# Attention decode block: other loads for W_o's last head, V, W_gate and x, and group ends placed one step later

## Chip, cores and metric

The kernel runs on one core of one Trainium2 chip. The metric is the device time of one execution in microseconds (us). Three runs gave 660.15, 661.10 and 661.72 us, so the median is 661.1 us.

## What is computed

One decode step (one token) of a pre-norm block for a batch of two: attention over a cache, then a gated MLP.

```python
h  = x + attention(layernorm(x))           # x: [2, 1, 512]
#   q = x @ wq: 32 heads of 128;  k_cache, v_cache: [2, 32, 8192, 128], bf16
#   p = softmax(q k^T * 128**-0.5);  o = p v;  attention = o @ wo     (wo: [4096, 512])
h2 = h + (relu(n @ W_gate) * (n @ W_up)) @ W_down      # n = layernorm(h), F = 1376
```

The two caches hold 268 MB and every byte is used once. With the weights, 281 MB are read.

## The kernel before, in words

**Tiling.** K and V are read in tiles of four heads of one batch element ("quads"): 128 partitions x 64 KB, 8.4 MB each. There are 16 such groups. Steps 0 to 14 take one quad each (Q is step 14, `LASTQ`); the last group is cut into two pairs of heads, p0 and p1, whose tiles have 4.2 MB.

**Buffers.** Three buffers of 64 KB a partition (`bufs`) serve all tiles in rotation. V of step i+1 goes where K of step i was, and is issued by SyncE (SP) after `scores(i)` on VectorE (DVE). K of step i+2 goes where V of step i was, and is issued after `values(i)` on TensorE (PE). At the end the same buffers take W_o, W_gate, W_up and W_down.

**A step.** `scores_pe` does the last 24 to 32 of the step's 256 blocks of keys with PE and ScalarE (ACT). `products` (L378, DVE) multiplies the other blocks with q in place, and `scores` (L396, L398, DVE) sums them by halving. `largest_of_own` and ACT (L418) make the exponentials, and `place_own` (L423, DVE) lays them out in `pgq`. `values` (L449) is 64 matmuls with V.

**Groups of heads.** After steps 3, 7, 11 and 14 (`groups`), `diagonals` collects up to 16 heads' outputs in `o_ps`. `close(i)` ends a group one step later. It multiplies the sums out (`own_sums`, L299, DVE), adds them over partitions (`sums`, L308, PE), takes the reciprocal (`shares`, L312, DVE) and scales (`normalise`, L316, DVE). In step i+1 it stands behind `place_own` and the first eight matmuls of `values`. For group 11, in step 12, `spread` (L484, DVE) and `lay_rows` (L495, L497) follow. They turn heads 0 to 15 into the rows that W_o's set 0 needs.

**The order on each engine** is the order of the code (`tc.manual_schedule()`). So a DVE instruction that waits for PE holds all DVE work behind it.

**Loads.** All loads but x are issued by SP. Each load takes the next of eight completion semaphores, and its issue waits until the load eight places before it has landed. At the end SP issues in this order: V of p0, W_o set 0, V of p1 in four pieces (L588), W_o sets 1 to 3, W_o's heads 30 and 31 in one load (L591), W_gate in two, W_up in two, W_down in seven (L619). The lines that the change replaces there:

```python
load_tile(A_v_cache, p1, p1.vt, pieces=4)
...
nc.sync.dma_start(
    out=wo[:, HM * D:Hq * D].rearrange("p (h n) -> p h n", n=D),
    in_=_dram(A_wo, HM * Dh * D, [[D, P], [Dh * D, Hq - HM], [1, D]]),
)
```

**After the last step** come the pairs: `values_cols(p1)` (L472), `attend_set` (L505) and `attend` for heads 30 and 31 (L512). Then come the second layernorm, W_gate and W_up (L673), the residual (L701), W_down (L712), `y` (L717), a transpose and the store (L723).

Of the kernel before, what the change touches and what calls it, by code (L numbers as in the profile page):

```python
# [18 lines left out]
def _dram(t, offset, dims):  # L19
    return bass.AP(tensor=t.tensor, offset=t.offset + offset, ap=[list(d) for d in dims])  # L20
# [3 lines left out]
def kernel(  # L24
# [13 lines left out]
    nc = tc.nc  # L38
    P = nc.NUM_PARTITIONS
    B, Sq, D = A_x.shape  # L40
    _, Hkv, Sk, Dh = A_k_cache.shape
    Hq = A_wq.shape[1] // Dh
# [26 lines left out]
    HM = 30  # L69
# [53 lines left out]
    xr = bufs[2][0:B, HALF + Hq * Dh:HALF + Hq * Dh + D]  # L123

    wo = bufs[0][:, HALF:TILE]
# [32 lines left out]
    Q = LASTQ  # L158

    def load_tile(cache, s, dst, pieces=1):  # L160
        h = NH * s.g + (0 if s.quad else 2 * s.k)
        n = s.nt * Dh
        w = n // pieces
        for k in range(pieces):
            nc.sync.dma_start(
                out=dst[:, k * w:(k + 1) * w], in_=_dram(cache, (s.b * Hkv + h) * Sk * Dh + k * w, [[n, P], [1, w]]),
            )
# [18 lines left out]

    with tc.manual_schedule():

        nc.scalar.dma_start(out=xr, in_=_dram(A_x, 0, [[D, B], [1, D]]))
        nc.sync.dma_start(out=bufs[2][:, 0:HALF], in_=_dram(A_wq, 0, [[KC * Hq * Dh, P], [1, KC * Hq * Dh]]))  # L190
        load_tile(A_k_cache, steps[0], steps[0].kt)
        load_tile(A_v_cache, steps[0], steps[0].vt)
# [6 lines left out]
            out=nscale, in_=nscale, compare_op=ALU.not_equal, fill=-SCALE,  # L199
# [5 lines left out]
            out=ident_f, in_=ident_f, compare_op=ALU.not_equal, fill=1.0,  # L205
# [4 lines left out]
            out=sel, in_=sel, compare_op=ALU.not_equal, fill=1.0,  # L210
# [9 lines left out]
            out=pick, in_=pick, compare_op=ALU.not_equal, fill=1.0,  # L220
# [24 lines left out]
        for g0 in range(0, NQ, 4):  # L245
            for n0 in range(NH * g0 * Dh, NH * (g0 + 4) * Dh, 4 * Dh):
                q_ps = ps2.tile([B, 4 * Dh], f32, tag="o")
                for c in range(KC):
                    nc.tensor.matmul(  # L249
                        out=q_ps, lhsT=xn[:, c, :], rhs=wq_sb[:, c, n0:n0 + 4 * Dh], start=(c == 0), stop=(c == KC - 1),  # L250
# [46 lines left out]
        def own_sums(i):  # L297
            b, g0, n = groups[i]
            nc.vector.tensor_tensor(  # L299
                out=zc[:, b, g0:g0 + n, :], in0=_free(zs, b * NQ + g0, [[1, n], [0, NH]]),  # L300
                in1=_free(own, 0, [[0, n], [1, NH]]), op=ALU.mult,
            )

        def sums(i):

            _, _, n, z = heads(i)
            z_ps[i] = ps.tile([P, n], f32, tag="mx", name="z_ps")
            nc.tensor.matmul(out=z_ps[i], lhsT=ones, rhs=z, start=True, stop=True)  # L308

        def shares(i):  # L310
            rzs[i] = small.tile([P, heads(i)[2]], f32, tag="rz", name="rz", bufs=2)
            nc.vector.reciprocal(out=rzs[i], in_=z_ps[i])  # L312

        def normalise(i):
            b, h0, n, _ = heads(i)
            nc.vector.tensor_tensor(out=ocol[:, h0:h0 + n, b], in0=o_ps[i][:, 0:n], in1=rzs[i], op=ALU.mult)  # L316

        def close(i):
            own_sums(i)
            sums(i)  # L320
            shares(i)
            normalise(i)

        scols = {
            i: qrep[:, c0:c0 + n].rearrange("p i d -> p (i d)").bitcast(f32)
# [48 lines left out]
        def products(s, t0=0, t1=None):  # L374

            n = (s.nv if t1 is None else t1) - t0
            kv = _free(s.kt, t0 * Dh, [[Dh, n], [1, Dh]])
            nc.vector.tensor_tensor(out=kv, in0=kv, in1=_free(s.qr, 0, [[0, n], [1, Dh]]), op=ALU.mult)  # L378
# [9 lines left out]
        def scores(s):  # L388

            scol = scols[s.i]  # L390
            width = Dh
            while width > 8:
                half = width // 2
                lo = _free(s.kt, s.na * Dh, [[Dh, s.nv - s.na], [1, half]])
                hi = _free(s.kt, s.na * Dh + half, [[Dh, s.nv - s.na], [1, half]])
                nc.vector.tensor_tensor(out=lo, in0=lo, in1=hi, op=ALU.add)  # L396
                width = half
            nc.vector.tensor_reduce(  # L398
                out=scol[:, s.na:s.nv], in_=_free(s.kt, s.na * Dh, [[Dh, s.nv - s.na], [1, 8]]), axis=AXIS.X, op=ALU.add,
            )  # L400
            pms[s.i] = small.tile([P, 1], f32, tag="pm", name="pm", bufs=2)
            nc.vector.tensor_reduce(out=pms[s.i], in_=scol, axis=AXIS.X, op=ALU.max)  # L402
# [40 lines left out]
        def values(s, u0, u1):  # L443

            r = slice(32 * (s.g % 4), 32 * (s.g % 4) + s.nh * VG)
            if u0 == 0:
                pv_ps[s.i] = ps2.tile([P, VG * Dh], f32, tag="o", name="pv_ps")
            for u in range(u0, u1):
                nc.tensor.matmul(  # L449
                    out=pv_ps[s.i][r, :], lhsT=s.pg[:, u].rearrange("p j t -> p (j t)"),  # L450
                    rhs=s.vt[:, u * VG * Dh:(u + 1) * VG * Dh], start=(u == 0), stop=(u == s.nt // VG - 1),
                )
            if u1 == s.nt // VG:
                nc.scalar.activation(out=pv[r, :], in_=pv_ps[s.i][r, :], func=ACT.Copy)  # L454
# [24 lines left out]
        def spread(k, b):  # L479

            h0, n, _ = SETS[k]
            nq = Dh // n
            sp = qrep[:, B * k + b, :]
            nc.vector.tensor_tensor(  # L484
                out=_free(sp, 0, [[nq, n], [1, nq]]), in0=_free(ocol, h0 * B + b, [[B, n], [0, nq]]),
                in1=_free(quot[n], 0, [[0, n], [1, nq]]), op=ALU.mult,
            )
            return sp

        def lay_rows(k, sps, scalar=False):  # L490

            r = SROWS[k]
            or_ps = ps.tile([P, B, r], f32, tag="mx")
            for b in range(B):
                nc.tensor.matmul(out=or_ps[:, b, :], lhsT=sps[b], rhs=rest[r], start=True, stop=True)  # L495
            if scalar:
                nc.scalar.activation(out=orow[k], in_=or_ps.rearrange("p b c -> p c b"), func=ACT.Copy)  # L497
            else:
                nc.vector.tensor_copy(orow[k], or_ps.rearrange("p b c -> p c b"))
# [18 lines left out]
        for i in range(Q):  # L518
            s = steps[i]
            scols[i] = small.tile([P, s.nt], f32, tag="scol", name="scol")  # L520
            scores_pe(s)
            place_q(steps[i + 1])
            products(s)
            scores(s)
            if i == Q - 2:
                load_tile(A_k_cache, steps[Q], steps[Q].kt)
            else:
                load_tile(A_v_cache, steps[i + 1], steps[i + 1].vt)
            if i == Q - 1:
                scores_pe(steps[Q])  # L530
            largest_of_own(s)
            if i == Q - 1:
                products(steps[Q], 0, NEXT)
            place_own(s)
            half = s.nt // VG // 2
            ahead = 8 if i - 1 in groups else 0
            if ahead:
                values(s, 0, ahead)
                close(i - 1)
            if i == 12:  # L540
                sps = [spread(0, b) for b in range(B)]
                values(s, ahead, 2 * ahead)
                ahead *= 2
                lay_rows(0, sps, scalar=True)
            values(s, ahead, half)
            if i == Q - 1:
                load_tile(A_k_cache, steps[Q + 1], steps[Q + 1].kt)
            values(s, half, 2 * half)
            if i in groups:
                diagonals(i)  # L550
            if i + 2 < Q:
                load_tile(A_k_cache, steps[i + 2], steps[i + 2].kt)
            elif i == Q - 2:
                load_tile(A_v_cache, steps[Q - 1], steps[Q - 1].vt)
            else:
                load_tile(A_k_cache, steps[Q + 2], steps[Q + 2].kt)


        s, p0, p1 = steps[Q:]
# [7 lines left out]
        def load_set(k):  # L567
            h0, n, at = SETS[k]
            nc.sync.dma_start(
                out=wo[:, at * D:(at + n) * D], in_=_dram(A_wo, h0 * Dh * D, [[n * D, P], [1, n * D]]),  # L570
            )
# [13 lines left out]
            at[1] = min(at[1] + 11, p0.na)  # L585

        scores_pe(p0, values_and_sums)
        load_tile(A_v_cache, p1, p1.vt, pieces=4)  # L588
        for k in range(1, len(SETS)):
            load_set(k)  # L590
        nc.sync.dma_start(  # L591
            out=wo[:, HM * D:Hq * D].rearrange("p (h n) -> p h n", n=D),
            in_=_dram(A_wo, HM * Dh * D, [[D, P], [Dh * D, Hq - HM], [1, D]]),
        )
        scores(p0)

# [13 lines left out]
        scores_pe(p1, lambda: next(turns)())  # L610
        act_sums(p1)
        products(p1, 48)
        for w, src, c, n in ((0, B_W_gate, 0, 2), (0, B_W_gate, 2, 2), (1, B_W_up, 0, 2), (1, B_W_up, 2, 2)):
            nc.sync.dma_start(
                out=wgu[:, w, c:c + n].rearrange("p c f -> p (c f)"), in_=_dram(src, c * F, [[KC * F, P], [1, n * F]]),
            )
# [137 lines left out]
```

## Time and profile before

| | before |
|---|---|
| median of three runs | 661.1 us |
| time of the profiled execution | 660.24 us |
| its span, first to last instruction | 658.5 us |
| share of the span busy: PE, DVE, ACT, POOL | 53%, 85%, 19%, 1% |
| busy share of the loads' queue (16 transfer engines) | 99.0% |
| HBM read | 281.09 MB, 427 GB/s over the span |
| mean granted TensorE clock | 0.763 of full speed |

Times in the profile are counted from the first instruction. The chain of work that ended last goes back from the last instruction to whatever released each step. A load's landing is the last mark that its transfer engines set on its semaphore. A load of 128 partitions has 16 such marks, one for each engine.

### The profile page before, as it was taken

How to read it: one execution, taken by the hardware profiler on the slowest of the kernel's cores; microseconds unless marked ns; L12 is line 12 of the kernel's file. 1: busy time of each engine (PE TensorE's matmuls, PEld its weight loads, DVE VectorE, ACT ScalarE, POOL GpSimd, SP SyncE). 2: the span in 40 equal slices, each digit the busy share in tenths (PEclk: the TensorE clock that was granted, in tenths of full speed). 3: DMA queues.
4: the chain of work that ended last, by engine and by line, in shares of the span. 5: the costliest groups of instructions: out<-in, count | busy, mean ns of one | idle time of the engine just before them, and what ended most of it. 6: DMA issues, size and time to landing. Idle time of an engine off the chain costs nothing.

```text
span 658.5 us, 5118 instructions
## 1 busy us (share of the span) xinstructions
PE 349.5 (53%) x2123; PEld 159.0 (24%) x2123; DVE 557.5 (85%) x248; ACT 123.1 (19%) x335; POOL 7.0 (1%) x35
## 2 busy tenths in 40 slices
PE   2530924709175380926538092562909458191997
PEld 1220311304022130312214031221403224030456
DVE  2399697988979799897979979896997969999981
ACT  1130030300203030030302103030210304201870
POOL 3000000000000000000000000000000000000000
PEclk9875876958678595877959587695958869686895
DMA  9999999999999999999999999999999999999997
GB/s 382 446 443 446 402 431 438 446 446 396 442 438 439 434 427 430 438 430 435 438 426 443 426 438 431 430 439 442 422 430 431 438 443 426 430 429 425 424 417 278
DMA packets 7946, 281.40 MB, mean 427 GB/s; under 512 B 882, under 2 KB 1780, under 8 KB 2804
## 3 DMA queue, kind: packets, MB, share of 16 engines
q1 hardware_dynamic: 7920, 281.09, 99.0%
q8 instruction: 16, 0.26, 0.1%
q14 instruction: 6, 0.05, 0.0%
q10 hardware_dynamic: 4, 0.00, 0.0%
HBM read 281.09 MB, written 0.00 MB: 427 GB/s over the span
## 4 chain that ended last, share of the span: by engine, by line
DVE 52%; DMA 29%; PE 18%; issue 1%; ACT 1%; SPq 0%; DVEq 0%; ACTq 0%
DMA tile<-in_A_k_cache_dram 29%; DVE tile L378 23%; DVE tile L396 22%; PE pv_ps L449 15%; DVE scol L398 3%; DVE pgq L423 1%; ACT ecol L418 1%; DVE pm L402 1%; DVE qrep L398 1%; PE o_ps L472 1%; DVE pm L413 0%; PE z_ps L308 0%; PE att_ps L505 0%; PE d_ps L701 0%; DVE hmax L415 0%
## 5 line engine op out<-in xcount | busy, mean ns | idle before, releaser
L449 PE MATMUL pv_ps<-tile,pgq 128*16 128x512 bf16 x960 | 240.7, 416 | 240.8 <-DVE pgq L423 227.8
L378 DVE TENSOR_TENSOR tile<-tile,qrep 128x29696 bf16<-128x29696 bf16 (+3 forms) x16 | 232.4, 14522 | 36.9 <-DMA tile<-in_A_k_cache_dram 36.9
L396 DVE TENSOR_TENSOR tile<-tile 128x14848 bf16<-128x14848 bf16 (+7 forms) x68 | 236.5, 3477 | 2.3
L449 PEld LDWEIGHTS <-pgq 128*16 128x16 bf16 x960 | 90.6, 96 | 379.9 <-DVE pgq L423 239.7
L353 ACT ACTIVATE tile<-t_ps 128x1024 bf16<-128x1024 bf16 x53 | 52.6, 1022 | 16.6 <-PE t_ps L352 16.1
L454 ACT ACTIVATE pv<-pv_ps 16x512 f32<-16x512 f32 (+1 forms) x16 | 9.4, 590 | 232.5 <-PE pv_ps L449 232.5
L418 ACT ACTIVATE ecol<-scol,nmax 128x256 bf16<-128x256 f32 x14 | 7.1, 508 | 201.0 <-DVE nmax L417 201.0
L352 PE MATMUL t_ps<-ident,tile 128*128 128x128 bf16 x424 | 31.7, 226 | 16.5 <-DMA tile<-in_A_k_cache_dram 16.5
L343 PE MATMUL row_ps<-tile,qz 128*24 128x512 bf16 (+1 forms) x98 | 29.6, 383 | 18.9 <-ACT tile L353 18.9
L352 PEld LDWEIGHTS <-tile 128*128 128x128 bf16 x424 | 25.4, 102 | 31.4 <-DMA tile<-in_A_k_cache_dram 17.1
L398 DVE TENSOR_REDUCE scol<-tile 128x232 f32<-128x1856 bf16 (+1 forms) x14 | 28.9, 2068 | 0.5
L423 DVE TENSOR_TENSOR pgq<-ecol,ownb 128x1024 bf16<-128x1024 bf16 x15 | 10.4, 692 | 10.3 <-ACT ecol L418 10.3
L384 ACT ACTIVATE tile<-tile 128x128 bf16<-128x128 bf16 x60 | 17.6, 294 | 1.9 <-DVE tile L378 1.9
L378 DVE TENSOR_TENSOR tile<-tile,qpair 128x4096 bf16<-128x4096 bf16 (+3 forms) x4 | 15.5, 3884 | 0.0
L252 DVE CAST tile<-q_ps 2x512 bf16<-2x512 f32 x8 | 5.4, 679 | 10.9 <-PE q_ps L249 10.9
L343 PEld LDWEIGHTS <-qz 128*24 128x24 bf16 (+1 forms) x98 | 7.8, 92 | 28.3 <-issue 22.8
L249 PE MATMUL q_ps<-tile,xn 128*2 128x512 bf16 x32 | 10.2, 486 | 8.4 <-DMA tile<-in_A_wq_dram 8.4
L370 ACT ACTIVATE scol<-sc_ps 32x24 f32<-32x24 f32 (+1 forms) x56 | 11.7, 210 | 7.7 <-PE sc_ps L365 7.2
L365 PE MATMUL sc_ps<-ident_f,tile 24*128 24x24 f32 (+2 forms) x68 | 7.2, 221 | 11.0 <-ACT tile L361 11.0
L361 ACT ACTIVATE tile<-row_ps 24x512 f32<-24x512 f32 (+2 forms) x17 | 10.0, 586 | 13.5 <-PE row_ps L343 13.5
L312 DVE RECIPROCAL rz<-z_ps 128x16 f32<-128x16 f32 (+1 forms) x4 | 0.9, 236 | 12.6 <-PE z_ps L308 12.6
L384 ACT ACTIVATION_READ_ACCUMULATOR tile<-tile 128x1 f32 x60 | 11.2, 187 | 0.0
(130 smaller groups left out, 130.8 us busy)
## 6 DMA issues: line engine op xcount, KB each, us to landing
tile<-in_A_k_cache_dram SPq DMA_DIRECT2D x2, 4096.0 KB, 21.7
tile<-in_A_wq_dram SPq DMA_DIRECT2D x1, 4096.0 KB, 12.4
tile<-in_A_v_cache_dram SPq DMA_DIRECT2D x1, 4096.0 KB, 19.4
tile<-in_A_v_cache_dram SPq DMA_DIRECT2D x4, 1024.0 KB, 20.5
tile<-in_A_wo_dram SPq DMA_DIRECT2D x1, 2048.0 KB, 23.8
tile<-in_B_W_gate_dram SPq DMA_DIRECT2D x2, 688.0 KB, 13.6
tile<-in_B_W_up_dram SPq DMA_DIRECT2D x2, 688.0 KB, 12.4
tile<-in_A_wo_dram SPq DMA_DIRECT2D x1, 1024.0 KB
```

The source lines that it names most:

```text
L249: nc.tensor.matmul(out=q_ps, lhsT=xn[:, c, :], rhs=wq_sb[:, c, n0:n0 + 4 * Dh], start=(c == 0), stop=(c == KC - 1),)
L343: nc.tensor.matmul(out=row_ps, lhsT=z, rhs=s.kt[:, (nv + c0 + k) * Dh:(nv + c0 + k + 4) * Dh], start=(u == 0), stop=(u == U - 1),)
L352: nc.tensor.transpose(t_ps[:, k, :], s.kt[:, t * Dh:(t + 1) * Dh], ident)
L353: nc.scalar.activation(out=s.kt[:, (nv + c0) * Dh:(nv + c0 + TPC) * Dh], in_=t_ps.rearrange("p t s -> p (t s)"), func=ACT.Copy,)
L370: nc.scalar.activation(out=scols[s.i][r, nv:s.nt].rearrange("p (u t) -> p t u", t=4), in_=sc_ps[r, :, :, j], func=ACT.Copy,)
L378: nc.vector.tensor_tensor(out=kv, in0=kv, in1=_free(s.qr, 0, [[0, n], [1, Dh]]), op=ALU.mult)
L384: nc.scalar.activation(out=kv, in_=kv, func=ACT.Copy, accum_out=scols[s.i][:, t:t + 1])
L396: nc.vector.tensor_tensor(out=lo, in0=lo, in1=hi, op=ALU.add)
L398: nc.vector.tensor_reduce(out=scol[:, s.na:s.nv], in_=_free(s.kt, s.na * Dh, [[Dh, s.nv - s.na], [1, 8]]), axis=AXIS.X, op=ALU.add,)
L418: nc.scalar.activation(out=ecol, in_=scols[s.i], func=ACT.Exp, scale=SCALE, bias=nmax, accum_out=zs[:, s.b, s.g:s.g + 1],)
L423: nc.vector.tensor_tensor(out=s.pg, in0=_free(ecol, 0, [[VG, s.nt // VG], [0, NH], [1, VG]]), in1=_free(ownb, 0, [[0, s.nt // VG], [VG, NH ...
L449: nc.tensor.matmul(out=pv_ps[s.i][r, :], lhsT=s.pg[:, u].rearrange("p j t -> p (j t)"), rhs=s.vt[:, u * VG * Dh:(u + 1) * VG * Dh], start= ...
```

## The change

1. x is loaded in four pieces of 256 elements each, instead of one load; ACT issues them.
2. The ends of groups are taken apart. In the step after the group, `own_sums` stands before the first eight matmuls of `values` and `sums` behind them. `shares` and `normalise` come one step later still, behind `products`. `spread` and `lay_rows` for heads 0 to 15 move from step 12 to step 13, behind `products` too.
3. V of p1 is one load of 4.2 MB instead of four, and W_gate one instead of two.
4. W_o's head 30 is a load of its own over 16 transfer engines. Head 31 is another whose source is written as 4 x 32 rows, so that four engines carry it.

```diff
-        nc.scalar.dma_start(out=xr, in_=_dram(A_x, 0, [[D, B], [1, D]]))
+        for b in range(B):
+            for k in range(2):
+                nc.scalar.dma_start(
+                    out=xr[b:b + 1, k * D // 2:(k + 1) * D // 2], in_=_dram(A_x, b * D + k * D // 2, [[D, 1], [1, D // 2]]),
+                )
...
-        def close(i):
-            own_sums(i)
-            sums(i)
-            shares(i)
-            normalise(i)
...
             products(s)
+            if i - 2 in groups:
+                shares(i - 2)
+                normalise(i - 2)
+            if i == Q - 1:
+                lay_rows(0, [spread(0, b) for b in range(B)], scalar=True)
             scores(s)
...
             if ahead:
+                own_sums(i - 1)
                 values(s, 0, ahead)
-                close(i - 1)
-            if i == 12:
-                sps = [spread(0, b) for b in range(B)]
-                values(s, ahead, 2 * ahead)
-                ahead *= 2
-                lay_rows(0, sps, scalar=True)
+                sums(i - 1)
             values(s, ahead, half)
...
-        load_tile(A_v_cache, p1, p1.vt, pieces=4)
+        load_tile(A_v_cache, p1, p1.vt)
...
+        nc.sync.dma_start(out=wo[:, HM * D:(HM + 1) * D], in_=_dram(A_wo, HM * Dh * D, [[D, P], [1, D]]))
         nc.sync.dma_start(
-            out=wo[:, HM * D:Hq * D].rearrange("p (h n) -> p h n", n=D),
-            in_=_dram(A_wo, HM * Dh * D, [[D, P], [Dh * D, Hq - HM], [1, D]]),
+            out=wo[:, (HM + 1) * D:Hq * D], in_=_dram(A_wo, (HM + 1) * Dh * D, [[P // 4 * D, 4], [D, P // 4], [1, D]]),
         )
...
-        for w, src, c, n in ((0, B_W_gate, 0, 2), (0, B_W_gate, 2, 2), (1, B_W_up, 0, 2), (1, B_W_up, 2, 2)):
+        for w, src, c, n in ((0, B_W_gate, 0, 4), (1, B_W_up, 0, 2), (1, B_W_up, 2, 2)):
```

## Prediction

> **What bounds the kernel now.** I read the page first: the rows of the transfer engines over 40 slices of the span, and the loads' queue.
>
> ```profile
> DMA  9999999999999999999999999999999999999997
> GB/s 382 446 443 446 402 431 438 446 446 396 442 438 439 434 427 430 438 430 435 438 426 443 426 438 431 430 439 442 422 430 431 438 443 426 430 429 425 424 417 278
> q1 hardware_dynamic: 7920, 281.09, 99.0%
> ```
>
> The 16 engines carry data in every slice, and 281 MB at this rate fill the span. A step that computes faster cannot make the stream shorter. In the trace's landing marks, the first engine to finish a cache tile does so every 19.31 or 19.32 us (476.82, 496.14, 515.46, 534.79, 554.11), so the queue is never empty. Only the last microseconds are open: the stream's end and the computing that comes to its end at the same time. So next the chain of waits, from step 12 on:
>
> ```profile
> 471.74 27.44 DMA tile<-in_A_k_cache_dram
> 499.21 15.10 DVE tile L378
> ...
> 533.77 3.58 PE pv_ps L449 x8
> 537.36 0.56 PE z_ps L308 x2
> 537.93 0.27 DVE rz L312
> 538.23 0.18 DVE ocol L316
> 538.40 0.40 DVE qrep L484 x2
> 538.80 15.02 DVE tile L378
> ...
> 639.74 1.81 PE o_ps L472 x64
> ...
> 654.25 1.33 PE d_ps L712 x44
> 655.60 0.18 DVE y L717
> ```
>
> Up to 499.21 a K tile decides. From 538.8 to 638 nearly every piece is DVE's, then PE's to the end. Between them stands the wait that the change attacks: DVE has nothing to do from 533.80 to 537.93, because its reciprocal needs `sums`, which stands behind eight matmuls on PE. The page's row of that line, and two loads by their lines: K of step 13 and the last piece of W_down.
>
> ```profile
> L312 DVE RECIPROCAL rz<-z_ps 128x16 f32<-128x16 f32 (+1 forms) x4 | 0.9, 236 | 12.6 <-PE z_ps L308 12.6
> ...
> L165 SPq DMA_DIRECT2D tile<-in_A_k_cache_dram x1: 328/328/328, 511.7 to 511.7; - x1
> DMA to landing us min/median/max: 26.0/26.0/26.0
> ...
> L619 SPq DMA_DIRECT2D tile<-in_B_W_down_dram x1: 328/328/328, 649.5 to 649.5; - x1
> DMA to landing us min/median/max: 5.7/5.7/5.7
> ```
>
> K of step 13 lands at 511.74 + 26.0 = 537.8 (mark: 537.78), so the wait cost its successor only about 1 us. The last W_down piece lands at 655.26 by its mark. PE's 44 matmuls from 654.25 take 30 ns each, and the four that read this piece begin at 655.46. Stream and computing end 0.2 us apart.
>
> The engines don't end together. First and last mark of some loads:
>
> ```
> K, step 0       31.74 ...  32.42      K, step 13     534.79 ... 537.78
> V, step 0       51.05 ...  53.30      last W_down    651.90 ... 655.26
> last W_down, all 16: 651.90 .97 652.51 .55 .57 .75 653.12 .16 | 654.29 .32 .32 .35 .47 .50 .70 655.26
> ```
>
> The lag comes from 16 fetches of instructions (16 KB each, 0.9 us on one engine, queue q8). They go round eight engines, the same one being hit by fetch 1 and fetch 9. So at the end eight engines are late and eight have 1.1 to 3.4 us to spare.
>
> **Group ends.** Of the waits at L312, 3.7 us lie in step 4 and 4.1 us in each of steps 8 and 12. In steps 4 and 8 they fall where DVE would wait for K anyway: in step 4 `products` of step 5 begins at 228.40, and its K had landed at 227.26. A start 1.1 us sooner issues V of step 6 sooner (261.55 now), while the first engine is busy until 263.93. Worth 0; if that cover were gone, 1.1 us each. In step 12 `products` of step 13 begins at 538.72 in the timeline. It will begin at 537.81, just after its K (step 12's began 0.03 us after its landing): -0.91 us. But `shares`, `normalise` and two `spread` (0.79 us from 537.93 to 538.72) now stand behind `products`, on the same DVE chain: +0.79. Together -0.12 us, between -0.91 (if they found a gap) and +0.2 (one more small DVE instruction's time, 0.17). PE and ACT get `lay_rows` after `scores_pe(13)`, which ends at 557.1; the rows are ready by 554. Behind it waits `scores_pe(14)`, 0.2 us later at most, and its result is needed by DVE's maximum at 605.4: free. What is late next is K of p0, landed 605.37 and taken by DVE at 607.85.
>
> **x in four.** Three more issues on ACT at 0.52 us. Behind them queue ACT's table load and warm-up, which waits for POOL until 6.51 anyway. x lands near 3.9 instead of 2.36, its layernorm takes 4.9 us and ends by 9; PE needs it with W_q, at 13.19. Cost 0, with 4 us to spare; a late x would delay K of step 1, for which the stream has 24 us.
>
> **Fewer loads.** V of p1 in four pieces passes the first engine in 636.60 - 626.79 = 9.81 us; V of p0, as many bytes in one load, in 621.93 - 612.24 = 9.69: -0.12. W_gate takes 3.34; at the V pieces' rate (64 KB an engine in 2.45) its 86 KB take 3.30: -0.04. One load for V must wait for what its last piece waited for, 618.21; the stream then still has work until 626.79. It lands at 639.35 instead of 639.47, and PE takes it from 639.74. That is the thinnest cover here, 0.3 us after computing is 0.12 earlier. With three loads fewer, SP's waits for a semaphore's last load come sooner or at the same load (W_down's pieces stay eight behind the same ones). Cost 0.
>
> **W_o's heads 30 and 31.** Now 16 rows of 1 KB per engine in 0.68 us, 42.5 ns a row. After: 8 rows everywhere (0.34), and 32 rows (1.36) on four engines. So twelve engines gain 0.34 and four lose 1.02. With the fewer loads: -0.50 on twelve, +0.86 on four. The extra issue on SP (0.38 us) is 10 us ahead of the engines.
>
> The Trainium skill (DMA: Bandwidth & Descriptors, "Rules for kernel authors") speaks against this edit: an outermost size below 16 confines the whole load to that many engines. Its section "Why a DMA increments its semaphore by 16 and not by 1" adds that these are the lowest-numbered ones. The store at the end, 8 rows, shows 8 packets of data, which agrees. No row numbers the engines.
>
> If the four are among the early eight, the last landing goes from 655.26 to 654.76, and the chain decides: its last matmuls at 655.34. If they are among the late, it goes up to 656.12. I take the first, as the load sizes are known and the chain is then what counts.
>
> **Sum.** Chain -0.12; stream 0.5 earlier and not needed. 660.24 - 0.12 = 660.1 for the profiled execution, which lies 0.86 under the median; so 661.0 for the median. Its own range is 660.2 to 661.7, the scatter of the three runs. What can be told from no change is about 0.2%, 1.3 us.
>
> **Rivals.**
> *Four late engines.* Marks of the late eight plus 0.86: the last landing is 655.2 to 656.1 and the last matmuls wait up to 0.7 us. 661.1 to 661.8, say 661.5. For it: nothing tells which engines are lowest. Within 0.2% still.
>
> *Faster: the wait in step 12 is worth more.* If K of step 13 landed with its first engine's 534.79, `products` would begin at 534.82, and the chain gains 538.72 - 534.82 - 0.79 = 3.1 us: 658.0. It counts over 0.2% from a landing before 536.6, that is a lag below 1.8 us. For it: the lag was about 2 us at the tiles landing until 440 us. Against: the fetches come with the program, and the timed runs are not shorter than the profiled one. The stream allows it only if its end has less lag as well; with the lag as it is, no gain can pass 0.7 us.
>
> *Slower: single rows on four engines are dear.* The last engine to finish, alone by then, took its last seven 1 KB rows 105 ns apart instead of 43. At that pace head 31 takes 32 x 0.105 = 3.4 us on its four engines, 3.0 more than its 8 rows now. Were they late ones, the last landing is 655.26 - 0.16 + 3.0 = 658.1, 2.6 us after 655.46: 663.7. It decides over 0.2% from about 63 ns a row on late engines; early ones have at least 2.1 us to spare and would need 86 ns for any loss. Against: the slow rows are 7 of some 900, and head 31 goes through while all engines work.
>
> *The change doesn't do what it says*: head 31 over all 16 engines. Then stream -0.16, and the chain still gives 661.0, as forecast.
>
> **Numbers.** Forecast, with head 31 on early or on all engines: 0.47. Four late engines, within 0.2%: 0.15. Faster by over 0.2%: 0.20, of which most is the first rival and some is what one profiled execution may hide. Slower by over 0.2%: 0.18, the dear rows or a late engine hit by one more fetch (0.9 us on top of 0.7). So faster 0.20, same 0.62, slower 0.18. The range takes the forecast's scatter and the four late engines whole, and reaches 1.2 us down and 1.4 us up into the others: 659.8 to 662.4, with 2 in 10 left outside.
>
> **What would show it.** Right: no idle time of DVE before L312 except in the tail; `products` of step 13 within 0.1 us of its K; four small DVE pieces behind it; the last W_down landing near 654.8; PE never waiting for DMA after 639. Wrong: PE idle before L472 or L712 with a DMA as releaser, the marks of four engines moved by over 1 us, or K of step 13 landing well before 537.8.

## The result, and the profile after

| | before | after |
|---|---|---|
| median of 21 runs each | 661.0 us | 659.8 us |
| shortest to longest | 659.77 to 662.18 | 659.55 to 660.67 |
| ratio | | 0.9984, 95% interval 0.9978 to 0.9990 |
| profiled execution, its span | 660.24, 658.5 us | 660.26, 658.5 us |

The change saves 0.16%, about 1 us. That is within the 0.2% that I called no change and at the lower edge of the range, but it is nine times the 0.12 us of my sum. The two profiled executions are equally long: that of before is a short one of its kernel, that of after a long one of its own. The shortest runs differ by 0.2 us; the long ones, up to 662.2, have gone. So the gain must be looked for in what makes executions long, not in the difference of two spans. One later run, of `e3_x`, took 713.88 us at a mean granted clock of 0.55 and is left out of the numbers below.

The row of `products` in the page of before (the row of L312 stands in the prediction):

```profile
L378 DVE TENSOR_TENSOR tile<-tile,qrep 128x29696 bf16<-128x29696 bf16 (+3 forms) x16 | 232.4, 14522 | 36.9 <-DMA tile<-in_A_k_cache_dram 36.9
```

The page of after: the queue's rows, then two rows of groups (L376 is `products`, L316 the reciprocal):

```profile
DMA  9999999999999999999999999999999999999996
GB/s 382 446 443 442 406 431 438 446 442 423 418 442 435 442 435 414 446 426 443 438 422 439 434 427 442 442 419 442 422 442 435 426 439 430 434 435 418 423 425 259
q1 hardware_dynamic: 7360, 281.09, 98.9%
...
L376 DVE TENSOR_TENSOR tile<-tile,qrep 128x29696 bf16<-128x29696 bf16 (+3 forms) x16 | 232.4, 14525 | 46.8 <-DMA tile<-in_A_k_cache_dram 46.8
...
L316 DVE RECIPROCAL rz<-z_ps 128x16 f32<-128x16 f32 (+1 forms) x4 | 0.9, 230 | 0.7 <-PE z_ps L312 0.7
```

DVE's wait for `sums` has fallen from 12.6 to 0.7 us. Of the 11.9 us, 9.9 come back as a longer wait for K (36.9 before, 46.8 now). By these rows alone the wait was only exchanged. The chain of waits, from step 12 on:

```profile
509.99 27.48 DMA tile<-in_A_k_cache_dram
537.49 15.09 DVE tile L376
552.59 0.18 DVE rz L316
552.79 0.18 DVE ocol L320
552.96 0.40 DVE qrep L482 x2
...
639.53 1.77 PE o_ps L470 x64
...
654.29 1.33 PE d_ps L711 x44
655.64 0.18 DVE y L716
```

`products` of step 13 begins 0.02 us after its K landed (mark 537.47), and the four small DVE pieces stand behind it, as forecast. The last load, W_down, by its line:

```profile
L618 SPq DMA_DIRECT2D tile<-in_B_W_down_dram x1: 328/328/328, 649.2 to 649.2; - x1
DMA to landing us min/median/max: 5.0/5.0/5.0
```

It lands at 654.20, 1.1 us sooner than before. But its matmuls start at 654.29, no sooner: the tail is still set by computing.

### The profile page after: what moved, and what is told of

Read it like the earlier page. It is cut to its first block, busy times and chain, and to the rows that moved or that the text cites. A ratio compares the mean times of both kernels' runs of the same rounds, so it can differ in the third digit from the quotient of the medians.

```text
span 658.5 us, 5121 instructions
## 1 busy us (share of the span) xinstructions
PE 351.4 (53%) x2123; PEld 159.9 (24%) x2123; DVE 557.2 (85%) x248; ACT 123.0 (19%) x335; POOL 6.3 (1%) x35
## 3 DMA queue, kind: packets, MB, share of 16 engines
q1 hardware_dynamic: 7360, 281.09, 98.9%
## 4 chain that ended last, share of the span: by engine, by line
DVE 43%; DMA 32%; PE 23%; ACT 1%; issue 1%; ACTq 0%; DVEq 0%
DMA tile<-in_A_k_cache_dram 30%; DVE tile L376 19%; DVE tile L394 18%; PE pv_ps L447 18%; DVE scol L396 2%; DMA tile<-in_A_x_dram 2%; PE q_ps L253 1%; DVE pgq L421 1%; PE att_ps L503 1%; ACT ecol L416 1%; PE o_ps L470 1%; DVE pm L400 1%; DVE qrep L396 0%; PE t_ps L350 0%; ACT pgp L434 0%
## 5 line engine op out<-in xcount | busy, mean ns | idle before, releaser
L376 DVE TENSOR_TENSOR tile<-tile,qrep 128x29696 bf16<-128x29696 bf16 (+3 forms) x16 | 232.4, 14525 | 46.8 <-DMA tile<-in_A_k_cache_dram 46.8
L376 DVE TENSOR_TENSOR tile<-tile,qpair 128x4096 bf16<-128x4096 bf16 (+3 forms) x4 | 15.5, 3884 | 0.0
L363 PEld LDWEIGHTS sc_ps<-ident_f,tile 24*128 24x128 f32 (+2 forms) x68 | 5.5, 137 | 19.4 <-ACT tile L359 19.4
```

The costliest lines, as they stand in the source:

```text
L363: nc.tensor.transpose(sc_ps[:, t].rearrange("p u j -> p (u j)"), rows[:, t * P:(t + 1) * P], ident_f[0:nh * U, 0:nh * U],)
```

## The experiments

Twelve kernels, five rounds each. Runs sent together share the runs of the kernel before (medians 660.52, 660.51 and 660.51 us). Two are the kernel before itself. They show what the comparison can tell: ratios of 1.0001 (0.9988 to 1.0013) and 1.0001 (0.9992 to 1.0010).

**Which part.** Three parts of the change, each put alone into the kernel before.

`e1_groups`, the group ends alone (the diff's edits of `close`, of the step and of `ahead`):

> The group ends alone (own_sums, sums, shares, normalise and the first rows of W_o one step later); loads and x as before. Theory A (the stream's end): most executions of the kernel before wait at the end for the last W_down, the group ends are worth the 0.12 us of the prediction: 660.9 against 661.0, with the wide scatter of before (659.8 to 662.2). Theory B (the group ends): DVE's wait in step 12 costs more in most executions than in the profiled one; then this alone gives 659.8 to 660.0 and the narrow scatter. Theory C (x): no change.

Measured: 659.71 (659.47 to 660.34), ratio 0.9984 (0.9974 to 0.9994). The whole gain and the narrow scatter.

`e2_loads`, the loads of the tail alone (V of p1, W_gate, heads 30 and 31):

> The loads of the tail alone: V of p1 and W_gate in one load each, heads 30 and 31 in two loads; group ends and x as before. Theory A: the last W_down lands about 0.5 us sooner (654.7 on the profile's scale), the end no longer waits for it: 659.8 to 660.1, scatter below 1.2 us. Theory B: 661.0, no change. Theory C: 661.0, no change.

Measured: 660.96 (659.71 to 661.79), ratio 0.9999 (0.9987 to 1.0011). Nothing, though its last W_down lands at 654.16, against 654.47, 655.26 and 655.48 in the three profiles of the kernel before. Theory A falls.

`e3_x`, the edit of x alone:

> x in four pieces alone. Theories A and B: 661.0, no change, as x comes late (near 12.8 us) but K of step 0 lands at 32.4 only. Theory C (a later start of q changes where instruction fetches and clock changes fall in the whole run): 659.8 to 660.2 with the narrow scatter.

Measured: 660.89 (659.92 to 662.96), ratio 1.0004 (0.9990 to 1.0017). Nothing; theory C falls.

`e4_same`, no edit:

> The kernel before once more, unchanged: ratio 1.000 within 0.1%, and a second profiled execution. If it is a longer one than 660.24, theory A expects PE to wait for W_down (L712) or the last mark of W_down to lie after 655.5; theory B a longer idle time ahead of L312 or a later start of products in step 13.

Measured: 660.84 (659.75 to 662.50). Its profiled execution took 661.13. Neither sign appeared: the last W_down mark is at 655.48, PE does not wait for it, and DVE's idle time before L312 in step 12 is 4.13 us as ever. It is longer because K of step 12 lands at 499.96 instead of 499.18, and all that follows comes 0.8 us later. Of this, 0.2 us is in the first mark (496.33, before 496.14) and 0.6 in the last engine's lag behind it.

**Which group.** Group 11's end lies on the chain of waits, so I had looked there only.

`f1_group11`:

```diff
             products(s)
+            if i == Q - 1:
+                shares(i - 2)
+                normalise(i - 2)
+                lay_rows(0, [spread(0, b) for b in range(B)], scalar=True)
...
-            if ahead:
+            if ahead and i == 12:
+                own_sums(i - 1)
+                values(s, 0, ahead)
+                sums(i - 1)
+            elif ahead:
                 values(s, 0, ahead)
                 close(i - 1)
-            if i == 12:
...
```

> Only group 11's end is moved (steps 12 and 13); groups 3 and 7 end as before, loads and x as before. Theory B1 (DVE's wait in step 12 is on the path in the longer executions): 659.7, narrow scatter, as with all groups moved. Theory B2 (the waits in steps 4 and 8 disturb the stream for the rest of the run): 660.5 to 661, wide scatter.

Measured: 660.72 (659.58 to 662.05), ratio 0.9997 (0.9987 to 1.0007). B1 falls.

`f2_groups37`, the same for groups 3 and 7, with step 12 left alone:

> Only the ends of groups 3 and 7 are moved; group 11 ends in step 12 as before. Theory B1: 660.5 to 661, wide scatter as before. Theory B2: 659.7 to 660.0 with narrow scatter.

Measured: 659.86 (659.52 to 660.48), ratio 0.9986 (0.9977 to 0.9994). As far as can be told, all of the gain comes from the two steps where the prediction counted it as nothing.

`f3_rows_later`, only `spread` and `lay_rows` moved to step 13:

> The reciprocal and the scaling stay in step 12 with DVE's wait; only spread and lay_rows go to step 13, so PE no longer waits for DVE in the middle of step 12's values. If that wait of PE is the cause (theory B3): 659.7, narrow. If DVE's wait is the cause (B1): 660.5 to 661, wide.

Measured: 660.89 (659.98 to 661.85), ratio 0.9998 (0.9989 to 1.0007). Nothing; B3 falls.

`f4_wait16`, a longer wait in step 12:

```diff
-            ahead = 8 if i - 1 in groups else 0
+            ahead = (16 if i == 12 else 8) if i - 1 in groups else 0
...
-                values(s, ahead, 2 * ahead)
-                ahead *= 2
+                values(s, ahead, ahead + 8)
+                ahead += 8
```

> The kernel before with 16 instead of 8 matmuls ahead of group 11's sums in step 12: DVE's wait grows by 8 matmuls of 0.21 to 0.42 us, 1.7 to 3.4 us. Theory B1: the whole of it on the time, 662.2 to 664. If the wait is hidden (as the prediction had it but for 1 us, products of step 13 starting at its K): also +1.7 to 3.4, since K of step 13 had landed 0.9 us before; hidden only if the executions that are long have their K late. Theory B2 or B3: less than 1 us more.

Measured: 662.29 (661.50 to 664.48), ratio 1.0030 (1.0017 to 1.0043). DVE's wait is 6.74 us instead of 4.13 and `products` of step 13 starts at 542.54. The wait in step 12 does cost when it grows; shortening it gains little (`f1_group11`), since K of step 13 lands 0.9 us before the start that it has. Part of the price is in the stream: V of step 14, whose issue follows `products` of step 13, is issued at 574.58, only 0.10 us before the first mark of the load ahead of it (574.68), and its own first mark comes 21.46 us after that one instead of 19.31. The profiled execution, 664.08, is a long one of this kernel.

**How much.** The wait of steps 4 and 8 doubled and halved.

`g1_wait16_37`:

```diff
-            ahead = 8 if i - 1 in groups else 0
+            ahead = (8 if i == 12 else 16) if i - 1 in groups else 0
```

> The kernel before with 16 instead of 8 matmuls ahead of the sums of groups 3 and 7 (steps 4 and 8); step 12 as before. Theory B2 (the late products of steps 5 and 9 issue V of steps 6 and 10 too late, and engines run dry): the issue comes 1.7 to 3.4 us later, the lead over K's first mark falls from 2.1 to 2.5 us to between -1 and 0.7, the first marks of those two V come 20.5 to 22 us after K's instead of 19.3 to 19.6, and the time goes to 662.0 to 664. Rival B1 (the steps' waits are covered, as the prediction had it): 660.5 to 661.0.

Measured: 664.14 (662.72 to 664.69), ratio 1.0052 (1.0039 to 1.0064).

`g2_wait4_37`, the same line with 4 in the place of 16:

> The kernel before with 4 instead of 8 matmuls ahead of the sums of groups 3 and 7; nothing else moved. Theory B2: DVE's wait falls to 2.4 us, it is free before K of steps 5 and 9 lands, the lead is 3.3 us or more, no engine runs dry: 659.7 to 659.9 with the narrow scatter, as with the group ends moved. Rival: something else in the moved instructions (their place behind products, PE's order) makes the gain; then 660.5 to 661.

Measured: 659.90 (659.35 to 660.70), ratio 0.9990 (0.9982 to 0.9999). One number in the kernel before gives the gain, up to what can be told; where the instructions stand makes no difference that these runs can tell.

`g3_after_less_37`, the changed kernel with groups 3 and 7 ended as before:

> The changed kernel with the ends of groups 3 and 7 put back as before (group 11, the loads and x stay changed). Theory B2: 660.5 to 661, wide scatter: all of the gain is undone. Rival (the parts help each other): 660.0 to 660.3.

Measured: 660.19 (659.65 to 661.75), ratio 1.0001 (0.9991 to 1.0011). The evidence is mixed. By the ratio all of the gain is undone, and the long executions are back: 4 of 11 over 661 us, against none of 12, 11 and 11 in `e1_groups`, `f2_groups37` and `g2_wait4_37`. The median alone lies in the range of the rival, that the parts help each other.

`g4_same_again`, no edit:

> The kernel before, unchanged, for one more profiled execution and the scatter. Theory B2: the longer this execution, the smaller the lead of V of step 6 or 10 (below 2.1 us in one over 660.5) and the later the first mark of that V after K's (over 19.5 us).

Measured: 660.45 (659.71 to 662.32). The profiled execution was a short one, 659.86, so the condition did not come up.

**What happens there.** DVE's timeline after step 4 in g1 and g2, and SP's issue of V of step 6 in both (start, length):

```profile
230.59 0.26 DVE L312 RECIPROCAL rz<-z_ps 128x16 f32<-128x16 f32 x1 [6.62 <-PE z_ps L308]
230.97 15.61 DVE L378 TENSOR_TENSOR tile<-tile,qrep 128x29696 bf16<-128x29696 bf16 x1
264.12 0.33 SPq L165 DMA_DIRECT2D tile<-in_A_v_cache_dram  x1
```

```profile
226.72 0.26 DVE L312 RECIPROCAL rz<-z_ps 128x16 f32<-128x16 f32 x1 [2.42 <-PE z_ps L308]
227.22 15.62 DVE L378 TENSOR_TENSOR tile<-tile,qrep 128x29696 bf16<-128x29696 bf16 x1
260.38 0.33 SPq L165 DMA_DIRECT2D tile<-in_A_v_cache_dram  x1
```

A start of `products` that is 3.75 us later makes the issue 3.74 us later: DVE is busy without a gap from one to the other. In g1 the queue then runs dry. The stretches 258 to 262, 262 to 266 and 266 to 270 us, g1 first and then g2 (columns: PE, PEld, DVE, ACT, POOL busy, PE clock, DMA share, GB/s):

```profile
258.00:262.00 4.00, 0.00 (x0) 0.00 (x0) 3.90 (x4) 0.00 (x0) 0.00 (x0) 0.50 0.98 426
262.00:266.00 4.00, 0.00 (x0) 0.00 (x0) 3.07 (x6) 0.60 (x2) 0.00 (x0) 0.50 1.00 360
266.00:270.00 4.00, 3.38 (x9) 1.04 (x10) 4.00 (x2) 0.00 (x0) 0.00 (x0) 0.50 0.60 262
```

```profile
258.00:262.00 4.00, 0.00 (x0) 0.00 (x0) 3.17 (x6) 0.49 (x2) 0.00 (x0) 0.50 1.13 492
262.00:266.00 4.00, 3.11 (x8) 1.01 (x9) 0.88 (x2) 0.11 (x2) 0.00 (x0) 0.53 0.87 377
266.00:270.00 4.00, 4.00 (x20) 1.71 (x19) 4.00 (x1) 0.00 (x0) 0.00 (x0) 1.00 1.02 442
```

A packet is counted where it starts, so single stretches scatter; over the three, g2 moves 437 GB/s and g1 349. At 437 the missing 88 GB/s are 2.4 us of 12. The trace's packet records, which have the start and the length of every row, show what happens in g1: the first packet of V of step 6 starts at 265.08, 0.96 us after the issue. The 16 engines stand idle for 1.1 us on average, and their first rows then take 2.73 to 3.35 us instead of 2.42. Together these make the 1.8 us that the landing marks show for this place.

The landing marks give the same for all kernels. The lead is the time from the issue of V of step 6 (and 10) to the first mark of the K before it. The step goes from K's first mark to V's, 19.31 when nothing is lost. The loss is the mean over the 16 engines, both places together: V's mean mark less K's less 19.30. The time of f4 has the loss at V of step 14 in it, which the table leaves out.

```
profiled execution        lead        step           loss   its time
before                 2.38  2.11  19.41  19.52     0.21   660.24
g4_same_again          2.33  2.11  19.55  19.53     0.31   659.86
e4_same                2.49  2.19  19.31  19.56     0.40   661.13
e2_loads               2.67  2.26  19.31  19.37     0.24   659.78
e3_x                   2.32  2.75  19.56  19.32     0.23   659.92
f1_group11             2.08  2.42  19.39  19.32     0.16   659.80
f3_rows_later          1.87  2.30  19.67  19.75     0.93   660.51
g3_after_less_37       2.13  2.63  19.65  19.31     0.59   659.97
f4_wait16              2.81  1.24  19.43  20.01     0.67   664.08
g1_wait16_37          -0.41 -0.04  21.76  21.36     3.60   664.14
g2_wait4_37            3.40  3.57  19.30  19.31     0.05   659.90
f2_groups37            3.56  3.37  19.32  19.32     0.07   659.83
e1_groups              3.33  3.33  19.31  19.31     0.15   659.90
after                  3.54  3.49  19.32  19.32     0.17   660.26
```

With a lead of 3.3 us or more nothing is lost in any of the four (the 0.1 in two of them is an instruction fetch; one is in e4's 0.40 too). All 11 leads of 1.87 to 2.38 us cost the first mark 0.1 to 0.4 us; of the six of 2.42 to 2.81 us one cost it 0.1. A lead of 1.24 us costs 0.7, and none costs 2. So it is not enough to issue before the first engines end the load ahead of it. A row of 64 KB takes an engine 2.42 us, and this fits a bound at the beginning of that load's last row. It is not shown: all rows here are of one size, so a fixed time would look the same, and in the kernel before seven engines had begun their last row when V of step 6 was issued, and six of them went on without a gap. g1's loss of 3.60 us is as much as its median is over the 660.51 of before (3.63 us).

**What stays open.** In the kernel before, the loss at these places in a profiled execution (0.21 to 0.40 us) is smaller than the gain, and the length follows it only loosely: of the three profiles of that kernel e4 is the longest with 0.40, but g4 with 0.31 is shorter than the first with 0.21, and g3 is short with 0.59. In e4 the last engine also lost 0.8 us in V of step 9 (the last marks of K and V are 20.09 us apart there), which is ahead of the second late issue. The executions of over 662 us, which have gone, were never among those profiled. That the waits of steps 4 and 8 make them is shown by what removes them (e1, f2, g2) and brings them back (g3). That they do it by the late issue is seen in g1's trace and inferred for the others; there is no trace of one that long. How an early loss on some engines becomes 1 to 2 us at the end is open.

## Why the prediction was right and wrong

**The time** lies on the edge of the range, and by size the forecast of no change to tell held. It held with a step that failed, and by luck: the term put at nothing came to 0.16%, just under the 0.2% that I had set.

**Group ends, steps 4 and 8: the term that was mis-sized.** I put it at 0, with the cover that "the first engine is busy until 263.93" when V of step 6 is issued, now at 261.55, and 1.1 us each if the cover were gone. The runs show about 1 us for both together (f2: -0.14%). The cover was measured to the end of the load in flight, as if any issue ahead of that end cost nothing. The runs show that it does cost: the leads were 2.38 and 2.11 us, leads of that size lost time at every place, and 3.3 us or more lost none. The evidence was in the trace: I listed five loads 19.31 or 19.32 us apart and concluded that the queue is never empty, and left out the three that follow the moved waits: V of step 6 at 19.41, V of step 10 at 19.52 and V of step 14 at 19.46.

**Group end, step 12.** -0.12 us: right within what can be told (f1: 0.9997). The first rival, faster by this wait, named the wrong step and another path, DVE's chain: K of step 13 never landed early. It landed at 537.1 to 538.6 in the eight profiles of kernels that keep the eight matmuls in this step, and at 541.1 in g1, where all is late.

**x in four.** No cost to tell, as said (e3). But x did not come at 3.9 us, and the 4 us to spare were not there. Each piece is one packet on one engine, and the four landed at 1.95, 7.89, 10.34 and 12.78: the later ones stand 2.45 us apart, two rows of W_q at 1.21 us each. x's users wait for it:

```profile
L191 ACTq DMA_DIRECT2D tile<-in_A_x_dram x4: 213/270/509, 0.7 to 1.8; - x4
...
  PE x_ps L239: 12.9, 1
```

q is some 2 us later (K of step 1 is issued at 28.74, not 26.89), and the cover of 24 us took it.

**Fewer loads.** The stream's end came sooner, by 1.1 us in the changed kernel's profile and by 0.3 to 1.3 us in e2's, and was not needed, as said: e2 measured nothing. The 0.5 us of the sum took head 31 to load four engines only, so it can't be compared term by term.

**Head 31.** The rival that the change does not do what it says is what happened: head 31's load has 16 marks, not 4. The 4 x 32 rows of the source follow each other without a gap, and in the built program they are one size of 128. So the rule of the Trainium skill (DMA: Bandwidth & Descriptors, "Rules for kernel authors"), that an outermost size below 16 confines a load, never came to bear, and no run here shows its price. The rivals of four late engines and of dear rows fell with it.

**What was to show it.** No idle time of DVE before L312 but in the tail: right. W_down near 654.8: it was 654.20. PE never waiting for a DMA after 639: right.

The changed kernel, e1, f2 and g2 measure the same, 659.7 to 659.9 us. One short lead is left in the changed kernel: V of step 14 is issued 2.71 us before the first mark of the load ahead of it, and its own comes after 19.39 us. No run was made to lengthen this lead, so what it is worth is open.

## What to carry to other kernels

Where a stream of loads is the bound, follow every delay of an engine to the issue that it releases, and ask how long before the end of the load in flight that issue comes. Here 3.3 us or more lost nothing, and less than 2.4 us did. The average share of the queue (99.0% with and 98.9% without the fault) cannot show a microsecond lost twice; the landing marks around the changed steps can, if all of them are listed. And where the medians differ but two profiled executions do not, compare the scatter, and run the parts of the change one at a time, before reading the traces.

## What the runs showed of the hardware

Small loads beside a bulk load on the same engine wait for its rows. The last three pieces of x took 2.45 us each, until 12.78 us. By the packet records their data start at 6.32, 8.77 and 11.22 us and the writes of their marks at 7.56, 10.00 and 12.45: the time of one row of W_q (1.21 us) passes before each. x in one load of two rows, issued at 0.74 us, had landed by 2.36.

A load that comes to engines with nothing to do starts late and slowly: in the two places of g1 its first packet starts 0.96 and 0.97 us after the issue, and nearly all of its first rows take 2.7 to 3.4 us instead of 2.42.

In this program the 4 x 32 adjacent rows were merged into 128, and the load ran on 16 engines, so writing it so did not choose its engines.
